# Value product of four head groups in one TensorE run, and attention weights loaded again for each chunk

## The chip, the cores and the metric

The kernel runs on one core of one Trainium2 chip. The metric is the time of one execution in microseconds (us), as the device measures it; the median of three runs of the kernel before is 558.66 us (558.55 to 558.71). A core has five engines that run side by side, each with an instruction stream of its own: TensorE (PE, matmuls; its weight loads are listed as PEld), VectorE (DVE), ScalarE (ACT), GpSimd (POOL) and SyncE (SP). Transfers are issued here by SP and POOL and carried by 16 DMA engines. TensorE writes to PSUM, which the kernel treats as four units of 1024 fp32 columns, two banks each.

## What is computed

```python
xn = layernorm(x)                                   # x: [1, 2048, 576]
qkv = xn @ wqkv                                     # 32 heads of 18
scores = q @ k^T * 18 ** -0.5, only for 0 <= i - j < 256
o = softmax(scores) @ v
s = concat(o) @ wo
h = sigmoid(xn @ w_gate) * (xn @ w_up)              # [2048, 4608]
g = silu(h @ w_down)
out = x + s * g
```

All tensors are bf16. The gated feed-forward part has eight times the width of the attention part and takes most of the matmul time.

## The kernel before

The 2048 rows are worked in four chunks of 512 (`NT`). For each chunk the builder makes operations, each with an engine, an estimated duration, dependencies and a priority: layer norm and transposition of the input (`build_ln`), the v projection (`build_v`), the q/k projection in five column groups (`build_qk`, `NQK` = 5), attention in eight head groups of four heads (`build_attn`), the output projection (`build_wo`), and the feed-forward part (`build_ffn`: 36 gate/up tiles `f1`, then `f2` in quarters of four tiles). `schedule` then puts all operations into one fixed order per engine with a model of durations and transfers, and `emit` writes the streams with the waits between them. The feed-forward matmuls of one chunk are laid between the attention work of that chunk and the next, so that TensorE has work while ACT and DVE treat the scores.

Nearly all matmuls are issued by `pair` (L122): two row tiles of 64 rows, each with 128 weight columns, side by side in the array.

*Attention of one head group.* Five score operations (`sc`) fill PSUM; ACT takes the exponential into a slot of the ring `expr` (L751, `NEX` = 12 slots), DVE multiplies the mask into it (L764). The exponentials stay transposed, keys on the partitions. The ring `qk` has `NQS` = 4 slots for the spread-out q and k of a head group.

*The value product.* After every second head group, `build_pv` makes one operation `pv` of 96 matmuls (64 in chunk 0, which has no earlier keys), L801. They are 64 rows by 19 columns of weights (18 values of v and a column of ones that yields the softmax sum), two row tiles by four column tiles: eight matmuls for each of 12 (8) blocks of keys. The results lie in one PSUM unit. DVE transposes each half out of PSUM (L819), takes the reciprocal of the sums (L822), multiplies (L823) and transposes back (L827); SP and POOL then move the rows into `oT` for the output projection. `ot1`, the fp32 transposed result, is a buffer of its own. There are four such runs in a chunk, 16 in the kernel.

*Weights.* wqkv and wo are loaded once, at the start or, for wo, after the first value run, and stay in SBUF (`wqk`, `wqkr`, `wv_sb`, `wvr`, `wo_sb`, `wor`); the last q/k group has its columns copied together into `wq4` by DVE. The 64 first rows of every weight (`...r`) lie apart from the other 512. Gate and up weights stream through a ring of four slots in every chunk; w_down is loaded in chunk 0 and stays.

*Order and PSUM.* `pool_s` (units 0 and 1) serves scores, projections and value products, `pool_f` (units 2, 3, 1) the feed-forward part. `schedule` picks for each engine the operation that can start first, with a small weight for its priority, and gives TensorE operations the unit that comes free first. `emit` places a wait ahead of an operation for each semaphore that is not yet known to have reached its value; what an instruction can't carry itself stands in the stream as an instruction that only waits.

The lines that matter below: L122 (`pair`), L801 (value product), L819 to L827 (its drain on DVE), L949 (the DVE half of an `f1` tile, which frees its PSUM unit), L1077 to L1174 (`schedule`).

Of the kernel before, what the change touches and what calls it, by code (L numbers as in the profile page):

```python
# [34 lines left out]
NQS = 4  # L35
NKX = 2
NEX = 12
OENG = ("SP", "POOL")
PV_ORDER = (0, 5, -4, -3, -2, -1, 1, 2, 3, 4, 6, 7)
TURN_NS = 265.0  # L40
BINS = (((-4, 0, 1), (1, 1, 5), (6, 6, 2)),
# [12 lines left out]
NXR = 2  # L54
# [135 lines left out]
class Op:  # L190
    __slots__ = ("eng", "est", "deps", "fn", "name", "prio", "start", "end", "tok", "needs_tok",
                 "nbytes", "slack", "idx", "succs", "cidx", "odeps", "acq", "lane", "filler", "space")

    def __init__(self, eng, est, fn, name, deps, prio, nbytes, odeps, acq):
# [30 lines left out]
        self.space = 0.0  # L225
        for d in self.odeps:
            assert d.eng == eng
# [22 lines left out]
class Builder:  # L250
# [17 lines left out]
    def op(self, eng, est, fn, name="", deps=(), prio=3, nbytes=0, odeps=(), acq=None):  # L268
        o = Op(eng, est, fn, name, deps, prio, nbytes, odeps, acq)
        o.cidx = len(self.ops)  # L270
        self.ops.append(o)
        for d in o.deps:
            d.succs.append(o)
        for d in o.odeps:
            d.succs.append(o)
        return o
# [12 lines left out]
    def alloc_memory(self):  # L289
# [30 lines left out]
        self.ot1, _ = seq("ot1", [P, 1, NT], f32)  # L320
# [4 lines left out]
        self.wqk, _ = seq("wqk", [P, KB - 1, 2, D])  # L325
        self.wqkr, _ = seq("wqkr", [P, D])
        self.wq4, _ = seq("wq4", [P, KB, 2, RD])
        self.wv_sb, _ = seq("wv_sb", [P, KB - 1, D])
        self.wvr, _ = seq("wvr", [P, D // 2])
        self.wo_sb, _ = seq("wo_sb", [P, KB - 1, D])  # L330
        self.wor, _ = seq("wor", [P, D // 2])
        self.qd, _ = seq("qd", [P, NQD, 2, NT])
        self.xr, _ = seq("xr", [P, NXR, D])
# [21 lines left out]
        self.pool_f = Pool("F", [2, 3, 1], last)  # L355

    def build_graph(self):
        self.r_xr = Ring(NXR, "xr")
# [6 lines left out]
        self.r_ot1 = Ring(1, "ot1")  # L365
# [21 lines left out]
        self.x_dma = {}  # L387
        self.op_wgr = {}
        self.q_slot = {}
        self.op_sp = {}  # L390
        self.sp_grp = {}
        self.hg_grps = {}
# [3 lines left out]
        for c in range(NC):  # L396
            self.build_ln(c)
            if c == 0:
                self.build_attn_consts()
            self.build_v(c)  # L400
            made = 0
            for hg in range(NHG):
                need = min(NQK, (4 * DH * (hg + 2) - 1) // P + 1)
                while made < need:
                    self.build_qk(c, made)
                    made += 1
                self.build_attn(c, hg)
            self.build_wo(c)
            self.build_ffn(c)

    def load_x(self, c, i=0):
# [8 lines left out]
        for _ in range(2):  # L420
            s_, d_ = self.r_xr.produce()
            slots.append(s_)
            dd += d_
        assert slots[1] == slots[0] + 1
        o = self.dma(self.xr[:, slots[0]:slots[0] + 2, :],
# [3 lines left out]
        for j in range(2):  # L429
            self.x_dma[st + j] = (o, self.xr[:, slots[j], :])  # L430
# [9 lines left out]
    def build_consts(self):  # L440
# [17 lines left out]
        wq, wk, wv = (self.wqkv[:, i * D:(i + 1) * D] for i in range(3))  # L458
        self.op_wqk = [self.load_nat(self.wqk[:, :, i, :], w, "dma:wqk", ("wqk", i), 5) for i, w in enumerate((wq, wk))]
        self.op_wqk += self.load_rem(self.wqkr[:, :], (wq, wk), "dma:wqkr", ("wqkr",), 5)  # L460
        for o in self.op_wqk:
            o.slack = 2500.0
        self.op_wv = [self.load_nat(self.wv_sb[:, :, :], wv, "dma:wv", ("wv",), 6)]
        self.op_wv += self.load_rem(self.wvr[:, :], (wv[:, 0:288], wv[:, 288:D]), "dma:wvr", ("wvr",), 6)
        for o in self.op_wv:
            o.slack = 5000.0
        self.op_wqk4 = [op("DVE", 420, lambda e: e.tensor_copy(self.wq4[:, 1:KB, :, :], self.wqk[:, :, :, 512:D]), "init:wq4",
                           deps=self.op_wqk, prio=2)]
        for t in range(2):
            for i in range(2):  # L470
                self.op_wqk4.append(op("DVE", 130, lambda e, t=t, i=i: e.tensor_copy(
                    self.wq4[ROWS[t], 0, i, :], self.wqkr[ROWS[1 - i], 512:D]), f"init:wq4:{t}{i}", deps=self.op_wqk, prio=2))

    def warm(self, n, dep, before, est):
# [5 lines left out]
        for i in range(n):  # L480
            w = self.op("PE", est, f_warm, f"warm:{i}", deps=[dep], prio=4, acq=None if before else h, odeps=[before])
# [27 lines left out]
    def build_ln(self, c):  # L509
# [3 lines left out]
        for i in range(BPC):  # L513
# [24 lines left out]
            sn, dn = self.r_xn.produce()  # L538
# [17 lines left out]
            if c:  # L556
                self.r_xr.release(i % 2, ap)
# [11 lines left out]
            tr = op("PE", KB * 29.5, f_tr, f"tr:{st}", deps=[ap, dup, self.op_ident, war], prio=0, acq=h)  # L569
# [37 lines left out]
    def halves(self, h, n):  # L607
        b = h.units[0] * 1024
# [6 lines left out]
    def build_qk(self, c, gi):  # L615
# [6 lines left out]
        gc = slice(gi * P, (gi + 1) * P)  # L622

        def lhs(r, t, k):
            if gi == 4:
                return self.wq4[r, k, :, :].rearrange("p i c -> p (i c)")
            return self.wqk[r, k - 1, t, gc] if k else self.wqkr[r, gc]
# [4 lines left out]
        pj = self.two("qk", f"{c}:{gi}", n, h, lhs, rhs, [self.op_xnT[c], self.op_wqk if gi < 4 else self.op_wqk4, dq], n)  # L632
# [8 lines left out]
        for u in range(H):  # L641
# [12 lines left out]
            for w, (dst, src) in enumerate(moves):  # L654
                o = self.dma(dst, src, n_ * 2 * NT * 2 // len(moves), f"dma:sp:{c}:{u}:{w}:{gi}", ("qk", par, gi),
# [3 lines left out]
                self.sp_grp.setdefault((c, gi), []).append(o)  # L659
                self.r_qd.release(sq, o)  # L660
            self.hg_grps.setdefault((c, hg), set()).add(gi)

    def two(self, kind, tag, est_n, h, lhs, rhs, deps, n, prio=1):
        lo = None
        for hi in range(2):
            def f(eng, hi=hi):
                return turn(eng, self.halves(h, n), lhs, rhs, hi)
            lo = self.op("PE", len(BLOCKS[hi]) * mm_ns(est_n), f, f"{kind}{hi}:{tag}", deps=[lo] if hi else deps, prio=prio,
                         acq=None if hi else h)
# [7 lines left out]
    def build_v(self, c):  # L677
        op = self.op
        xs = c % 2
        for i in range(BPC):  # L680
# [5 lines left out]
            vp = self.row_proj("v", st, h, lambda r, k, cols=cols: self.xnT[r, xs, k, cols], self.wv_sb, self.wvr,  # L686
                               [self.op_xnT[c][i], self.op_wv, war])
            self.xnT_rel[c].append(vp)
            self.op_v[st] = []
# [14 lines left out]
    def build_attn(self, c, hg):  # L704
        op = self.op
        qs = self.q_slot[(c, hg)][0]
        sp = [o for gi in sorted(self.hg_grps[(c, hg)]) for o in self.sp_grp[(c, gi)]]
# [18 lines left out]
        for vi, (specs, groups) in enumerate(zip(bins, masks)):  # L726
# [3 lines left out]
            def f_sc(eng, specs=specs, h=h):  # L730
                res = None
                outs = self.halves(h, NT)
                for ks, q0, nq in specs:
# [7 lines left out]
                    deps=[sp, kxo, self.r_ex.rel[self.r_ex.uses % NEX]], prio=1, acq=h, odeps=[self.last_vis])  # L741
# [30 lines left out]
        if hg % 2:  # L772
            self.build_pv(c, hg // 2)
        if (c, hg) == (0, 1):
            pv = self.op_pv[(c, hg)]
            self.op_wo_w = [self.load_nat(self.wo_sb[:, :, :], self.wo, "dma:wo", ("wo",), 8, [pv])]
            self.op_wo_w += self.load_rem(self.wor[:, :], (self.wo[:, 0:288], self.wo[:, 288:D]), "dma:wor", ("wor",), 8, [pv])

    def build_pv(self, c, pr):
        op = self.op  # L780
        pend, self.pend = self.pend, []
        hp = self.pool_s.hold()
# [3 lines left out]
        span = {ks: (max(ks, 0), min(ks + 5, SPC)) for ks in kss}  # L786

        def f_pv(eng):
            res = None
            outs = self.halves(hp, NT)  # L790
            for n, ks in enumerate(kss):
                q0, q1 = span[ks]
                cols = slice(q0 * SW, q1 * SW)
                for g, (hg, where, _) in enumerate(pend):
                    se = where[(ks, q0)]
                    assert all(where[(ks, q)] == se for q in range(q0, q1))
                    for t in range(2):
                        o = sub_pos(c, ks) * VSZ + (2 * hg + t) * VH
                        p0 = 32 * (2 * g + t)
                        for i in range(2):  # L800
                            res = eng.matmul(outs[i][p0:p0 + VH, cols], self.v_aug[ROWS[i], o:o + VH],  # L801
                                             self.expr[ROWS[i], se, t, cols], start=n == 0, stop=n == len(kss) - 1,
                                             tile_position=(64 * i, p0), skip_group_check=True)
            return res
        est = TURN_NS + sum(mm_ns((b - a) * SW) for a, b in span.values())
        pv = op("PE", est, f_pv, f"pv:{c}:{pr}", deps=[[m for _, _, rd in pend for m, _ in rd], vdeps], prio=1, acq=hp)
        for hg, _, rd in pend:
            self.op_pv[(c, hg)] = pv
            for se in sorted({se for _, se in rd}):
                self.r_ex.release(se, pv)  # L810
        for i in range(2):
            p1, d1 = self.r_ot1.produce()
# [5 lines left out]
            def f_t1(e, i=i, p1=p1):  # L818
                return e.transpose(self.ot1[:, p1, :], self.halves(hp, NT)[i])  # L819
            t1 = op("DVE", dve_ns(NT), f_t1, f"ot:{c}:{pr}:{i}", deps=[pv, d1], prio=1)  # L820
            hp.release(t1)
            rc = op("DVE", 255, lambda e, o1=o1: e.reciprocal(o1[:, :, DH], o1[:, :, DH]), f"rc:{c}:{pr}:{i}", deps=[t1], prio=1)  # L822
            on = op("DVE", dve_ns(NT // 32 * DH), lambda e, o1=o1, o2=o2: e.tensor_tensor(  # L823
                o2[:, :, 0:DH], o1[:, :, 0:DH], o1[:, :, DH:VH].broadcast_to([P, NT // 32, DH]), ALU.mult),
                f"on:{c}:{pr}:{i}", deps=[rc, d2, self.op_o2z], prio=1)
            self.r_ot1.release(p1, on)
            t2 = op("DVE", dve_ns(NT), lambda e, p2=p2, p3=p3: e.transpose(self.o2T[:, p3, :], self.o2[:, p2, :]),  # L827
                    f"ot2:{c}:{pr}:{i}", deps=[on, d3], prio=1)
# [26 lines left out]
    def build_wo(self, c):  # L855
        op = self.op
        last = []
        for i in range(BPC):
# [7 lines left out]
            wo = self.row_proj("wo", qb, h2, lambda r, k, cols=cols: self.oT[r, k, cols], self.wo_sb, self.wor,  # L866
                               [self.op_o[c], self.op_wo_w, war])
# [404 lines left out]
```

## Time and profile before

| | |
|---|---|
| median of three runs | 558.66 us |
| profiled execution, its own time | 558.58 us |
| span of its profile, first to last instruction | 557.2 us |
| instructions in the profile | 19237 |
| L801 matmuls | 1408, in 16 runs |
| L819 transposes out of PSUM | 32, 700 ns mean, 22.4 us in all |
| L949 | 144, 683 ns mean, 98.2 us in all |
| L751 exponentials | 160, 969 ns mean, 154.8 us in all |
| main DMA queue (q1) | 105960 packets, 60.68 MB, 40.1% of 16 engines |
| all DMA | 67.83 MB, mean 122 GB/s |

A row of the timeline gives the start and the length of a group of equal instructions in us, the engine, the line, the operation, what it writes and reads, the shape and how many there are. The length of a matmul row runs to the modelled end of its last matmul, and matmuls overlap in the pipeline; so what a stretch costs TensorE is read from start to start, not from the lengths. A bracket at the end gives the idle time of the engine before the row and what ended it.

### The profile page before, as it was taken

How to read it: one execution, taken by the hardware profiler on the slowest of the kernel's cores; microseconds unless marked ns; L12 is line 12 of the kernel's file. 1: busy time of each engine (PE TensorE's matmuls, PEld its weight loads, DVE VectorE, ACT ScalarE, POOL GpSimd, SP SyncE). 2: the span in 40 equal slices, each digit the busy share in tenths (PEclk: the TensorE clock that was granted, in tenths of full speed). 3: DMA queues.
4: the chain of work that ended last, by engine and by line, in shares of the span. 5: the costliest groups of instructions: out<-in, count | busy, mean ns of one | idle time of the engine just before them, and what ended most of it. 6: DMA issues, size and time to landing. Idle time of an engine off the chain costs nothing.

```text
span 557.2 us, 19237 instructions
## 1 busy us (share of the span) xinstructions
PE 552.6 (99%) x8342; PEld 339.1 (61%) x8342; DVE 328.4 (59%) x787; ACT 274.9 (49%) x379; POOL 210.1 (38%) x360
## 2 busy tenths in 40 slices
PE   8999999999999999999999999999999999999998
PEld 7454444677755545457886555645588754444787
DVE  5477788787568667674558857357567523333111
ACT  4245654443656655645656464565656433333201
POOL 5564456566245454440667444034382200000000
DMA  7988987931125535434121264234511035542010
GB/s 222 309 244 191 230 257 218 204 61 45 51 75 155 160 107 147 142 108 96 28 63 45 70 191 125 84 113 140 168 38 38 23 105 156 171 144 75 2 44 25
DMA packets 113468, 67.83 MB, mean 122 GB/s; under 512 B 18620, under 2 KB 111516, under 8 KB 113384
## 3 DMA queue, kind: packets, MB, share of 16 engines
q1 hardware_dynamic: 105960, 60.68, 40.1%
q0 software_dynamic: 7424, 5.92, 4.0%
q8 instruction: 66, 1.08, 0.8%
q14 instruction: 18, 0.15, 0.1%
HBM read 55.15 MB, written 2.36 MB: 103 GB/s over the span
## 4 chain that ended last, share of the span: by engine, by line
PE 98%; DVE 1%; DMA 0%; issue 0%; ACT 0%
PE ps L122 95%; PE ps L801 3%; DMA x<-in_A_x_dram 0%; DVE small L525 0%; DVE small L527 0%; DVE xnr L541 0%; PE ps L599 0%; DVE xnr L545 0%; ACT thf L1059 0%; DVE small L529 0%; DVE small L531 0%; DVE thf L1061 0%; DVE xf L1064 0%
## 5 line engine op out<-in xcount | busy, mean ns | idle before, releaser
L122 PE MATMUL ps<-xnT,wgs 64*128 64x512 bf16 (+1 forms) x2400 | 282.6, 368 | 0.2
L751 ACT ACTIVATE expr<-ps 128x1024 bf16<-128x1024 f32 (+4 forms) x160 | 154.8, 969 | 77.8 <-PE ps L122 77.2
L122 PEld LDWEIGHTS ps<-xnT,wgs 64*128 64x128 bf16 x2400 | 113.8, 94 | 115.1 <-DVE hT L949 1.6
L122 PE MATMUL ps<-wd_sb,hT 64*128 64x288 bf16 (+2 forms) x2448 | 156.7, 276 | 0.0
L949 DVE SCALAR_TENSOR_TENSOR hT<-tring,ps 128x512 bf16<-128x512 bf16 x144 | 98.2, 683 | 94.8 <-ACT tring L946 93.7
L946 ACT ACTIVATE tring<-ps 128x512 bf16<-128x512 f32 x144 | 86.1, 598 | 129.8 <-PE ps L122 127.6
L122 PEld LDWEIGHTS ps<-wd_sb,hT 64*128 64x128 bf16 x2448 | 112.5, 94 | 28.4
L279 POOL DMA_DIRECT2D qk<-qd x160 | 82.2, 521 | 119.8 <-PE ps L122 109.6
L764 DVE TENSOR_TENSOR expr<-expr,mask 128x128 bf16<-128x128 bf16 (+2 forms) x240 | 63.2, 297 | 62.1 <-ACT expr L751 61.6
L715 POOL TENSOR_SCALAR kx<-kprev,small 128x256 bf16<-128x256 bf16 x64 | 61.3, 967 | 28.2 <-PE ps L122 27.4
L122 PE MATMUL ps<-qk,kx 64*128 64x320 bf16 (+1 forms) x704 | 59.4, 254 | 0.0
L279 POOL DMA_DIRECT2D oT<-o2T x72 | 36.4, 513 | 58.7 <-DVE o2T L827 49.8
L122 PE MATMUL ps<-xnT,wgr 64*128 64x512 bf16 (+1 forms) x300 | 55.9, 367 | 0.0
L122 PEld LDWEIGHTS ps<-qk,kx 64*128 64x128 bf16 x704 | 31.2, 94 | 21.6 <-ACT expr L751 0.6
L122 PE MATMUL ps<-xnT,wqk 64*128 64x512 bf16 x256 | 32.6, 376 | 0.0
L819 DVE STREAM_TRANSPOSE ot<-ps 128x512 f32<-128x512 f32 x32 | 22.4, 700 | 11.6 <-PE ps L801 11.6
L715 DVE TENSOR_SCALAR kx<-qk,small 128x512 bf16<-128x512 bf16 x64 | 22.3, 378 | 4.7 <-PE ps L122 4.1
L122 PEld LDWEIGHTS ps<-xnT,wgr 64*128 64x128 bf16 x300 | 14.9, 94 | 16.6
L827 DVE STREAM_TRANSPOSE o2T<-o 128x512 bf16<-128x512 bf16 x32 | 22.7, 711 | 1.0
L637 DVE CAST qd<-ps 128x1024 bf16<-128x1024 f32 (+1 forms) x20 | 22.1, 1110 | 1.5 <-PE ps L122 1.5
L697 ACT ACTIVATE v_aug<-ps 64x288 bf16<-64x288 f32 x32 | 13.1, 409 | 17.3 <-PE ps L122 16.8
L801 PEld LDWEIGHTS ps<-expr,v_aug 64*19 64x19 bf16 x1408 | 17.2, 87 | 6.0 <-issue 3.3
(72 smaller groups left out, 291.5 us busy)
## 6 DMA issues: line engine op xcount, KB each, us to landing
wgs<-in_B_w_gate_dram SPq DMA_DIRECT2D x72, 256.0 KB, 3.4
wgs<-in_B_w_up_dram SPq DMA_DIRECT2D x72, 256.0 KB, 3.8
wd_sb<-in_B_w_down_dram SPq DMA_DIRECT2D x9, 576.0 KB, 6.3
qk<-qd POOLq DMA_DIRECT2D x100, 36.0 KB, 2.6
wgr<-in_B_w_gate_dram SPq DMA_DIRECT2D x36, 64.0 KB, 2.2
wgr<-in_B_w_up_dram SPq DMA_DIRECT2D x36, 64.0 KB, 2.4
xf<-in_A_x_dram SPq DMA_DIRECT2D x16, 144.0 KB, 2.9
out_dram<-xf SPq DMA_DIRECT2D x15, 144.0 KB, 1.8
```

Source lines behind the costliest of these rows:

```text
L122: res = eng.matmul(outs[i], lhs(ROWS[t], i), rhs(ROWS[t], i), start=start, stop=stop, tile_position=(64 * t, 0))
L279: o = self.op(eng, DMA_ISSUE_NS[eng], lambda e: e.dma_start(dst, src), name, deps, prio, nbytes=nbytes)
L637: return eng.tensor_copy(dst, self.both(h, n))
L697: return eng.activation(dst, src, ACTF.Copy)
L715: return e.tensor_scalar(self.kx[:, sx, pos:pos + n_ // SW, t, :], src.rearrange("p (s k) -> p s k", k=SW), self.half[:, t:t + 1], None, A ...
L751: return eng.activation(self.expr[:, se, :, lo * SW:NT], self.both(h, NT)[:, :, lo * SW:NT], ACTF.Exp, scale=SM_SCALE)
L764: return eng.tensor_tensor(e_, e_, m_, ALU.mult)
L801: res = eng.matmul(outs[i][p0:p0 + VH, cols], self.v_aug[ROWS[i], o:o + VH], self.expr[ROWS[i], se, t, cols], start=n == 0, stop=n == len( ...
L819: return e.transpose(self.ot1[:, p1, :], self.halves(hp, NT)[i])
L827: t2 = op("DVE", dve_ns(NT), lambda e, p2=p2, p3=p3: e.transpose(self.o2T[:, p3, :], self.o2[:, p2, :]), f"ot2:{c}:{pr}:{i}", deps=[on, d3 ...
L946: th = op("ACT", act_ns(NT), lambda e: e.activation(self.tring[:, st, :], bank(h, 0), ACTF.Tanh, scale=0.5), f"th:{c}:{ft}", deps=[pg, dt_ ...
L949: mu = op("DVE", dve_ns(NT), lambda e: e.scalar_tensor_tensor(self.hT[:, ft, :], self.tring[:, st, :], 1.0, bank(h, 1), ALU.add, ALU.mult) ...
```

## The change

Three things change together.

The value product is made once for four head groups (`PVG` = 4): two operations of 96 (64) matmuls that stand directly behind each other in TensorE's order (`then`), in a hold of two PSUM units from a pool `pool_v` over all four units. Both units are released when all four transposes of the two parts are done. There are two such runs in a chunk, eight in the kernel. `expr` has 20 slots instead of 12, and `ot1` now uses the same ring's numbering and the memory of the same slots. The priorities of L822 to L827 go from 1 to 2.

The scheduler counts TensorE's instructions as it places them (`at`, two for each matmul: its weight load and itself, given by `ni`). The first part of a value run is placed only where its middle would lie within 10 instructions (40 in chunk 0) of 193 past a multiple of 256 by this count.

The buffers of the weights and the input change as well: q/k weights are loaded for each column group of each chunk into a ring of two (`load_wq`), v and o weights share one buffer and are loaded for each chunk (`load_vo`), the separate input buffer `xr` goes (the input is loaded into `xnr` and normalised in place), and the ring of q/k slots has three instead of four. A q/k group is projected one head group later than before, and attention waits only for the moves of its own head group.

```diff
-NQS = 4
+NQS = 3
-NEX = 12
+NEX = 20
+NWQ = 2
+PVG = 4
+FETCH = 256
+FETCH_AT = 193
+FETCH_OFF = 10
+FETCH_OFF0 = 40
...
+        self.ot1 = nc.alloc_sbuf_tensor_at("ot1", [P, NEX, NT], f32, offset=zex)
...
+        self.pool_v = Pool("V", [0, 1, 2, 3], last)
...
-                need = min(NQK, (4 * DH * (hg + 2) - 1) // P + 1)
+                need = min(NQK, (4 * DH * (hg + 1) - 1) // P + 1)
...
+    def load_wq(self, c, gi):
+        sw, dw = self.r_wq.produce()
+        wq, wk = (self.wqkv[:, i * D:(i + 1) * D] for i in range(2))
+        w = P if gi < 4 else RD
+        both = self.wqkv[:, 0:2 * D].rearrange("r (i c) -> r i c", i=2)[:, :, gi * P:gi * P + w]
+        main = self.wqg[:, sw, :, 0:2 * w].rearrange("p k (i c) -> p k i c", i=2)
+        ds = [self.dma(main[:, :, i, :], both[RD:D, i, :].rearrange("(k p) c -> p k c", p=P), (D - RD) * w * 2, f"dma:wq:{c}:{gi}:{i}",
+                       ("wqg", sw, i), deps=dw, prio=5) for i in range(2)]
...
+    def load_vo(self, c, w, name, deps):
+        ds = [self.load_nat(self.wvo[:, :, :], w, f"dma:{name}:{c}", (name,), 6, deps)]
+        ds += self.load_rem(self.wvor[:, :], (w[:, 0:288], w[:, 288:D]), f"dma:{name}r:{c}", (name + "r",), 6, deps)
...
     def build_v(self, c):
+        wv = self.load_vo(c, self.wqkv[:, 2 * D:3 * D], "wv", [self.wo_last])
...
-        if hg % 2:
-            self.build_pv(c, hg // 2)
+        if hg % PVG == PVG - 1:
+            self.build_pv(c, hg // PVG)
...
+    def build_pv(self, c, run):
         op = self.op
         pend, self.pend = self.pend, []
-        hp = self.pool_s.hold()
+        hold = self.pool_v.hold(PVG // 2)
...
+        for n in range(PVG // 2):
+            pair2 = pend[2 * n:2 * n + 2]
...
+            est = (0.0 if n else TURN_NS) + sum(mm_ns((b - a) * SW) for a, b in span.values())
+            before = pv
+            pv = op("PE", est, f_pv, f"pv:{c}:{run}:{n}", deps=[] if n else deps, prio=1, acq=None if n else hold, odeps=[before],
+                    ni=16 * len(kss))
+            if before:
+                before.then = pv
+            else:
+                pv.off = 16 * len(kss) * (PVG // 2) // 2
...
+            self.build_o(c, run * (PVG // 2) + n, hold, n, pv)
+
+    def build_o(self, c, pr, hp, un, pv):
         for i in range(2):
-            p1, d1 = self.r_ot1.produce()
+            p1, d1 = self.r_ex.produce()
...
             def f_t1(e, i=i, p1=p1):
-                return e.transpose(self.ot1[:, p1, :], self.halves(hp, NT)[i])
+                return e.transpose(self.ot1[:, p1, :], self.halves(hp, NT, un)[i])
             t1 = op("DVE", dve_ns(NT), f_t1, f"ot:{c}:{pr}:{i}", deps=[pv, d1], prio=1)
             hp.release(t1)
...
     def build_wo(self, c):
+        wo_w = self.load_vo(c, self.wo, "wo", [self.v_last])
...
     def schedule(self):
+        at = 0
+        nxt = None
...
                 for o in cand:
+                    if e == "PE" and nxt is not None and o is not nxt:
+                        continue
+                    if o.off is not None:
+                        d = (at + o.off - FETCH_AT + FETCH // 2) % FETCH - FETCH // 2
+                        if abs(d) > (FETCH_OFF if o.off > FETCH // 2 else FETCH_OFF0):
+                            continue
...
             if o.eng == "PE":
+                at += o.ni
+                nxt = o.then
```

## The prediction

> **What bounds the kernel now.** I read the busy shares first, then the chain that ended last, then the matmuls around one value run in order of time, then the instruction fetches.
>
> ```profile
> PE 552.6 (99%) x8342; PEld 339.1 (61%) x8342; DVE 328.4 (59%) x787; ACT 274.9 (49%) x379; POOL 210.1 (38%) x360
> ...
> PE 98%; DVE 1%; DMA 0%; issue 0%; ACT 0%
> ```
>
> TensorE is busy all the time and is nearly all of the chain. No other engine passes 60%. So only what shortens or holes TensorE's own stream counts, and every moved load or drain is free as long as TensorE does not run out of work for it. The granted clock is 1.00 throughout. The program after has the same 8342 matmuls, so the gain can only be in how they follow each other.
>
> The rows at one value run in chunk 1 (L801) and at one in chunk 0:
>
> ```profile
> 162.68 1.03 PE L122 MATMUL ps<-xnT,wgs 64*128 64x512 bf16 x8
> 163.54 0.38 PE L122 MATMUL ps<-xnT,wgr 64*128 64x512 bf16 x2
> 163.85 1.34 PE L801 MATMUL ps<-expr,v_aug 64*19 64x320 bf16 x96
> 165.13 0.40 PE L122 MATMUL ps<-qk,kx 64*128 64x64 bf16 x6
> ...
> 62.54 1.03 PE L122 MATMUL ps<-xnT,wgs 64*128 64x512 bf16 x8
> 63.40 0.38 PE L122 MATMUL ps<-xnT,wgr 64*128 64x512 bf16 x2
> 63.71 1.01 PE L801 MATMUL ps<-expr,v_aug 64*19 64x320 bf16 x64
> 64.65 0.39 PE L122 MATMUL ps<-qk,kx 64*128 64x320 bf16 x4
> ```
>
> Read the starts. Four pairs of 512 columns take 163.54 - 162.68 = 0.86 us, so a pair costs 0.215 us (0.42 ns a column). The last pair before a run takes 0.31: the way into a run costs 0.095 us. The run itself takes 1.28 us from its first start to the next matmul in chunks 1 to 3, and 0.94 us in chunk 0. Its columns alone (2560 and 1920, eight tiles at a time) are 1.075 and 0.806 us at 0.42 ns. All twelve runs of chunks 1 to 3 take 1.27 to 1.28 us in the trace's records, all four of chunk 0 take 0.94.
>
> The loads of weights show why the way in costs something:
>
> ```profile
> 163.33 0.10 PEld L122 LDWEIGHTS ps<-xnT,wgr 64*128 64x128 bf16 x2
> 163.85 1.19 PEld L801 LDWEIGHTS ps<-expr,v_aug 64*19 64x19 bf16 x96 [0.42 <-issue]
> ```
>
> Elsewhere a weight load starts under the matmul before it. Here none starts until the array has changed from two tiles of 64x128 to eight of 64x32. That is the turn, paid 16 times now and 8 times after.
>
> **The change part by part.** *Fewer turns.* In the records the last block of 8 matmuls of a run takes 178 ns (144 in chunk 0) to the next matmul, 122 ns of it after its last matmul; followed by another block of the same tiles I expect 68 (28): the records show eight matmuls 8 to 9 ns apart once the queue is drained, 3 to 4 ns apart in chunk 0. That saves 110 (116) ns. With it go the 95 ns in, about 7 ns in the first block, and 10 ns at the second pair after a run. Against it, the second half of a joined run in chunks 1 to 3 starts with a drained queue, so its narrow blocks are bound by issue (28 ns becomes about 68): 35 ns back. A join saves 0.19 us in chunks 1 to 3 and 0.226 in chunk 0. There are 6 and 2 of them: 6 x 0.187 + 2 x 0.226 = 1.57 us. Bounds: only the way in, 8 x 0.095 = 0.76; everything over the bare columns (0.296 and 0.229 a join), 2.23.
>
> *The two-unit hold.* A joined run takes two of the four PSUM units and gives both back after its fourth L819 transpose (700 ns mean). In chunks 1 to 3 the next claimant stands 1.94 to 2.16 us of TensorE work behind the run (f1 halves of 0.86 and 1.08, f2 quarters of 0.49); in chunk 0, 2.45 and 3.02. The DVE order puts the four transposes together. They begin some 0.2 us after the first half of the run ends (1.2 us before the joined run does), or after the L949 before them, and need 2.9 us: released 1.9 to 2.1 us after the run. Two runs, the first of chunk 1 and the last of chunk 3, come about 0.13 us short; I charge 0.27 us. Behind the claimant queue only matmuls in TensorE's fixed order, so a late release is a hole. If one L949 (683 ns) slipped between the transposes, each of the six later runs would lose about 0.6. Bounds: 0 to 3.6.
>
> *Loads.* SP issues 456 transfers instead of 362, POOL the same 356. The weights of 2.7 MB come again in three chunks, 8 MB on 67.8, and q/k in rows of 256 B: some 20,000 more packets. A packet of the main queue costs 40.1% x 16 x 557 / 105960 = 34 ns of one of 16 engines, so the packets cost 11 us of all engines per chunk of 139 us, against a DMA share of 0.41 in 139 to 270 us and 0.37 in 270 to 400. In the first 60 us the share is 0.86, but there the queue now carries q/k in parts as they are needed, and f1 weights move up: counting bytes of the queue against its packet ends, f1 weights land 5 to 16 us ahead of their first matmul from 20 to 70 us. Hidden: 0. If that cover were gone, a stall would be of the order of one landing, 3.4 us for a gate weight. The o weights now wait for v's last matmul and v's for o's; v is due only at the next value run, tens of us later. In-place normalising and three q slots lengthen waits on SP and POOL, which TensorE does not see while the score order holds. The init copies to wq4 leave DVE (1 us, off the path).
>
> *Where the runs' middles really stand.* Queue q8 fetches TensorE's instructions:
>
> ```profile
> q8 instruction: 66, 1.08, 0.8%
> ```
>
> 66 fetches of 16 KB is one per 256 instructions over 2 x 8342 = 16,684 loads and matmuls plus 219 instructions that only wait. Set against the stream's position, the fetch times fit best with an edge at 193 past each multiple of 256 *if the waiting instructions are counted*. The scheduler's count `at` adds only `ni`, so it drifts; the program after holds 260 such waits. Counted in full, the eight middles lie +30, +34, +103, +135, -102, -56, -38 and -9 instructions from the nearest edge. So the change mostly does not do what it says: three runs (both of chunk 1, the first of chunk 2) hold two edges, 256 apart; the others one.
>
> What that costs depends on how far ahead blocks are fetched, which this trace does not show: its closest edges are about 4 us apart, and no run waits. In runs of the trace a fetch starts 1.1 to 1.6 us after the edge is passed and takes 0.9 to 1.4: landed after 2.0 to 2.7 us. TensorE, some 42 instructions behind its sequencer, needs 298 instructions x 6.1 ns = 1.8 us to use up what it has. If only one block is ahead, three runs lose 0.2 to 0.9 us each, 0.6 to 2.7 in all, about 1.7. If more are ahead, 0. I take 0, since in no row has TensorE waited for a block, even where a fetch came 5 us after its edge; but both ends stay in the range.
>
> The Trainium skill, "Runtime: NRT & Kernel Launch", section "Instruction fetch mechanics", says that blocks of 256 are prefetched in sequence and hidden because an engine issues no faster than about 20 cycles an instruction. The row speaks against the reason: 192 instructions in 1.28 us is 6.7 ns. The same section gives a buffer of two blocks in one sentence and 2,048 instructions for TensorE in another; by the first the sum would be the rival's below, by the second the forecast's.
>
> **Sum.** The profiled execution took 558.58 us (span 557.25 and 1.33 around it), 0.08 under the median of 558.66. 558.58 - 1.57 + 0.27 = 557.28; on the median 557.36, say 557.3.
>
> **The rivals.** *Turn gain eaten by fetch.* One block ahead, three runs short: 557.36 + 1.7 = 559.1 (558.0 to 560.1). For it: the landing times and the missed edges. Against it: no wait for a block in the trace. It is slower than before by over 0.2% from 0.8 us a run, that is from landings 2.6 us after the edge.
>
> *Slower: the drain behind a joined run.* Place: the first claim after each of the six runs of chunks 1 to 3. If one L949 stands ahead of a transpose the hole is about 0.6 us: 557.1 + 3.6 = 560.7. It decides from 0.45 us a run (1.57 + 1.1 over 6). For it: margins of 0 to 0.2 us, while one-unit runs left 3.0 to 4.3. Against it: the order puts the four transposes first.
>
> *Late loads.* 256 B rows land later than planned and TensorE waits once or twice for a q/k part: 557.4 + 1 to 2 = 558.9. Against it: the landing margins above.
>
> **How the numbers follow.** Forecast 0.52, fetch 0.30, drain 0.10, late loads 0.08. A measurement of this kernel can't tell less than about 0.2% (1.1 us) from no change. The forecast's own range is 556.4 to 557.9 and is beyond 0.2% with 0.45 of its 0.52. The fetch rival gives 0.03 faster, 0.17 the same, 0.10 slower; the drain 0.10 slower; late loads 0.05 same and 0.03 slower. Together: faster 0.48, same 0.29, slower 0.23. The range runs from 556.4 to 559.9, which leaves out the drain and the upper part of the fetch case.
>
> **What would show it.** Eight value runs: their first start to the next matmul near 2.47 us (twice 1.28 less 0.11 and 0.007, plus 0.035; 1.76 in chunk 0), and 0.31 before each. If the fetch rival is right, the three runs with two edges are longer by 0.2 to 0.9 us than the three others, with a gap near instruction 294 to 345 of 384, right where the second fetch lands. If the drain is, TensorE idles before the first score behind a run, released by L819's successor. Late loads would show as waits on a DMA. I am wrong if TensorE's busy time outside the value runs changes, or if a join saves under 0.1 us.

## The result, and the profile after

| | before | after |
|---|---|---|
| median | 558.68 us (558.55 to 558.89, 4 runs) | 566.08 us (565.75 to 569.93, 4 runs) |
| ratio, 95% interval | | 1.0148 (1.0104 to 1.0191) |
| span of the profile | 557.2 us | 564.8 us |

The change makes the kernel slower by about 7.4 us. The busy shares of after and the shares of the chain that ended last:

```profile
PE 553.2 (98%) x8342; PEld 340.6 (60%) x8342; DVE 324.4 (57%) x782; ACT 272.1 (48%) x379; POOL 207.8 (37%) x360
...
PE 97%; issue 1%; DVE 1%; DMA 0%; ACT 0%
```

TensorE does the same 8342 matmuls in nearly the same busy time (552.6 us before), so the loss is idle time between matmuls. "Issue" has grown from 0% to 1% of the chain: TensorE stood still, and nothing that the profile records was late. The view of the waits, by engine and line (what was waited for, us in total, times, longest), says where:

```profile
PE ps L816 <- issue: 6.2, 3, 2.8
```

L816 is the value product. Three waits, none of them for another engine. The timeline of TensorE at two joined runs without a wait (the second of chunk 2, the first of chunk 0) and at two of the three with one (first of chunk 1, second of chunk 1):

```profile
374.64 2.47 PE L816 MATMUL ps<-expr,v_aug 64*19 64x320 bf16 x192
377.05 1.04 PE L127 MATMUL ps<-xnT,wgs 64*128 64x512 bf16 x8
...
86.39 1.86 PE L816 MATMUL ps<-expr,v_aug 64*19 64x320 bf16 x128
88.19 1.04 PE L127 MATMUL ps<-xnT,wgs 64*128 64x512 bf16 x8
...
196.09 2.35 PE L816 MATMUL ps<-expr,v_aug 64*19 64x320 bf16 x172
201.27 0.37 PE L816 MATMUL ps<-expr,v_aug 64*19 64x256 bf16 x20 [2.82 <-issue]
201.57 1.05 PE L127 MATMUL ps<-xnT,wgs 64*128 64x512 bf16 x8
202.44 0.60 PE L127 MATMUL ps<-xnT,wgr 64*128 64x512 bf16 x2
202.84 1.92 PE L127 MATMUL ps<-xnT,wgs 64*128 64x512 bf16 x8
204.54 0.64 PE L127 MATMUL ps<-qk,kx 64*128 64x64 bf16 x6
...
254.53 2.11 PE L816 MATMUL ps<-expr,v_aug 64*19 64x320 bf16 x156
258.46 0.64 PE L816 MATMUL ps<-expr,v_aug 64*19 64x320 bf16 x36 [1.82 <-issue]
```

Read from start to start. A joined run takes 2.41 us where nothing holds it (2.56 as two runs before) and 1.80 in chunk 0 (1.88 before). The stalled ones stop behind 172 and 156 matmuls. Behind the longest stop there is a second loss: eight matmuls of 512 columns, which take 0.87 us from 201.57 to 202.44, take 1.70 from 202.84 to 204.54. The view by windows (us, busy time and count of PE, PEld, DVE, ACT and POOL, granted clock, DMA share, GB/s) has the reason:

```profile
201.40:206.00 4.60, 4.60 (x50) 1.99 (x37) 3.22 (x6) 1.37 (x2) 0.00 (x0) 0.63 0.01 4
```

The granted clock is 0.63 in this stretch; in the records it is 0.5 for one piece of 3.41 us, from 202.47 to 205.88, and 1.0 up to the end of the work otherwise.

The three stops, set against the fetches of TensorE's instructions (queue q8). "Passed" is when its sequencer passed the edge in the first half of the run, worked out from the position in the stream with the sequencer 42 instructions ahead of the matmuls; fetch and stop are rows of the trace, us; "stop" is the start of the last matmul ahead of it, and the last column counts the instructions of the run up to there, two for each matmul:

```
run            passed   fetch starts  landed   stop     goes on   stop lasts   at instruction
chunk 1, 1st   196.34   198.76        199.74   198.17   201.27    3.09         344 of 384
chunk 1, 2nd   254.55   255.70        256.96   256.34   258.46    2.12         312
chunk 2, 1st   313.12   314.27        315.39   315.10   316.97    1.87         294
```

The second edges of these runs were worked out beforehand at 345, 313 and 294. So each fetch brings the block behind the next edge, and TensorE stops at that edge until the block can be used, which is 1.5 to 1.6 us after it has landed.

What the half clock costs can be read from the starts: the work from 202.44 to 206.08 takes 3.63 us; its eight pairs of 512 columns at 0.215 us and its score operation at 0.22 take 1.94 at full clock, so 1.7 us are lost.

The time is nearly all accounted for: stops 7.03 us over what those matmuls cost otherwise, half clock 1.7, some more small holes 0.7, and 1.9 gained by the joins, 7.5 in all; the spans differ by 564.8 - 557.2 = 7.6.

### The profile page after: what moved, and what is told of

Its sections match the earlier page's. It is cut to its first block, busy times and chain, and to the rows that moved or that the text cites. A ratio compares the mean times of both kernels' runs of the same rounds, so it can differ in the third digit from the quotient of the medians.

```text
span 564.8 us, 19415 instructions
## 1 busy us (share of the span) xinstructions
PE 553.2 (98%) x8342; PEld 340.6 (60%) x8342; DVE 324.4 (57%) x782; ACT 272.1 (48%) x379; POOL 207.8 (37%) x360
## 4 chain that ended last, share of the span: by engine, by line
PE 97%; issue 1%; DVE 1%; DMA 0%; ACT 0%
PE ps L127 94%; PE ps L816 3%; DMA x<-in_A_x_dram 0%; DVE small L540 0%; DVE small L542 0%; DVE xnr L556 0%; PE ps L612 0%; DVE xnr L560 0%; ACT thf L1086 0%; DVE small L544 0%; DVE small L546 0%; DVE thf L1088 0%; DVE xf L1091 0%
## 5 line engine op out<-in xcount | busy, mean ns | idle before, releaser
L127 PEld LDWEIGHTS ps<-xnT,wgs 64*128 64x128 bf16 x2400 | 112.5, 94 | 116.9 <-issue 2.6
L127 PEld LDWEIGHTS ps<-wd_sb,hT 64*128 64x128 bf16 x2448 | 115.0, 94 | 26.8
L779 DVE TENSOR_TENSOR expr<-expr,mask 128x128 bf16<-128x128 bf16 (+2 forms) x240 | 64.9, 297 | 72.2 <-ACT expr L766 70.8
L730 POOL TENSOR_SCALAR kx<-kprev,small 128x256 bf16<-128x256 bf16 x64 | 59.9, 946 | 11.5 <-PE ps L127 10.6
L127 PE MATMUL ps<-xnT,wqg 64*128 64x512 bf16 (+1 forms) x320 | 37.8, 355 | 0.0
L844 DVE STREAM_TRANSPOSE ot<-ps 128x512 f32<-128x512 f32 x32 | 20.4, 688 | 16.8 <-PE ps L816 16.8
L816 PE MATMUL ps<-expr,v_aug 64*19 64x320 bf16 (+4 forms) x1408 | 19.3, 254 | 6.2 <-issue 6.2
L816 PEld LDWEIGHTS ps<-expr,v_aug 64*19 64x19 bf16 x1408 | 16.9, 86 | 10.3 <-issue 9.1
```

Of the source, the lines that this page charges most:

```text
L127: res = eng.matmul(outs[i], lhs(ROWS[t], i), rhs(ROWS[t], i), start=start, stop=stop, tile_position=(64 * t, 0))
L730: return e.tensor_scalar(self.kx[:, sx, pos:pos + n_ // SW, t, :], src.rearrange("p (s k) -> p s k", k=SW), self.half[:, t:t + 1], None, A ...
L779: return eng.tensor_tensor(e_, e_, m_, ALU.mult)
L844: return e.transpose(self.ot1[:, p1, :], self.halves(hp, NT, un)[i])
```

## The experiments

Theory A: two edges of the fetch blocks follow each other faster than a block can be fetched and made ready. Rivals: the joined run itself (its length, its hold of two PSUM units), the reloaded weights, and whatever else the rings moved.

**e1: the scheduler counts the instructions that only wait.** The whole change stays; only the count becomes right, so that each run's middle really lies on an edge.

```diff
-        at = 0
+        at = 2
...
+                        pick = o.acq.pool.pick(o.acq.n, max(free[e], ready_t[o.cidx]))
+                        extra = len(waits(o, pick[1])) // 2 if pick else 0
-                        d = (at + o.off - FETCH_AT + FETCH // 2) % FETCH - FETCH // 2
+                        d = (at + extra + o.off - FETCH_AT + FETCH // 2) % FETCH - FETCH // 2
...
-                at += o.ni
+                w_ = waits(o)
+                known.update(w_)
+                at += o.ni + len(w_) // 2
```

> The changed kernel with the scheduler's count made to include the instructions that only wait, so that the middles of all eight value runs lie within 10 instructions of an edge in chunks 1 to 3 and within 30 in chunk 0. Theory A (one block is fetched ahead, and a run with two edges stalls at the second): no gap over 0.2 us inside any value run, granted clock 1.00, and the eight joins save 6 x 0.25 + 2 x 0.19 = 1.9 us against the kernel before: 556.8 us, at most 557.6. Theory B (the loss comes from the weights that are loaded again and the smaller rings): still 563 to 566 us, since none of that is changed. Theory C (the two-unit hold): also still slow, with idle TensorE behind the runs.

Measured: 559.87 us (558.96 to 561.7, 12 runs), ratio 1.0017 (1.0008 to 1.0026). All eight joined runs go through without a stop, as this one of chunk 1 in the timeline of e1; but a stop remains behind another, in `f2`:

```profile
192.71 2.47 PE L816 MATMUL ps<-expr,v_aug 64*19 64x320 bf16 x192
195.11 1.04 PE L127 MATMUL ps<-xnT,wgs 64*128 64x512 bf16 x8
...
252.17 0.28 PE L127 MATMUL ps<-wd_sb,hT 64*128 64x288 bf16 x1
253.27 1.64 PE L127 MATMUL ps<-wd_sb,hT 64*128 64x288 bf16 x23 [0.82 <-issue]
```

About 6.2 of the 7.4 us come back by the count alone. The time is still 2.3 us above theory A's upper bound of 557.6: in the profile stand two stops behind runs (1.10 and 0.43 us) and some 3 us of small holes, which e7 comes back to. This profile is of the slowest of the twelve executions (561.7 us), so the median one holds less of them. The stop behind 252.17 is at the next edge after a run that ended at 250.25: the edge before it was passed in the middle of the run, at 248.83, the fetch started at 250.75 and landed at 251.82, and TensorE went on at 253.27, 1.45 us later. So the rule is not about runs: a block takes so long, whatever work reaches its edge first.

**e2: the reloads and rings alone.** Runs of two head groups as before, placed anywhere.

```diff
-PVG = 4
+PVG = 2
...
-                pv.off = 16 * len(kss) * (PVG // 2) // 2
+                pv.off = None
```

> The changed kernel with value runs of two head groups again (16 runs, one PSUM unit each, placed anywhere); the weights loaded again for each chunk, the rings and the priorities stay as changed. Theory A: 558.7 us, between 558.3 and 559.5, value runs of 1.28 and 0.94 us as before, clock 1.00. Theory B: 563 us or more. Theory C: 558.7.

Measured: 559.22 us (558.3 to 560.32, 12 runs), ratio 1.0006 (0.9997 to 1.0016). The reloads are not what costs 7 us. Their own price, 0.65 us by the medians, can't be told from nothing. The profile, of the slowest of the twelve (560.32 us), has two single waits. One fetch in its profile, outside the value runs, started 4.67 us after its edge and stopped TensorE for 0.64 us, 1.58 after landing to the next matmul. And one value run of chunk 0 waited 1.0 us for the mask product (L779), where the kernel before has no such wait.

**e3: as many edges as possible.** e1 with the target half a block further on, so that each of the six runs of chunks 1 to 3 holds two edges, some 68 and 324 instructions in.

```diff
-FETCH_AT = 193
+FETCH_AT = 193 + 128
```

> As e1_waits_counted, but every joined run is placed half a block off: all six runs of chunks 1 to 3 hold two edges (some 68 and 324 instructions in), the two of chunk 0 (256 instructions) one each. Theory A: six gaps of 1.9 to 3.1 us just ahead of instruction 324 of the run, 11 to 19 us together, and a stretch of 3.4 us at half clock (1.7 us lost) behind the longest ones: 568 to 585 us, middle 574. Theories B and C: no more than the changed kernel's 566.

Measured: 573.44 us (571.97 to 575.48, 4 runs), ratio 1.0261 (1.0236 to 1.0287). All six runs stop at the second edge, for 2.28, 2.25, 1.39, 2.71, 1.56 and 2.40 us. The longest, in the timeline of e3:

```profile
370.77 1.71 PE L816 MATMUL ps<-expr,v_aug 64*19 64x256 bf16 x118
374.90 0.63 PE L816 MATMUL ps<-expr,v_aug 64*19 64x320 bf16 x34 [2.41 <-issue]
375.46 0.40 PE L127 MATMUL ps<-qk,kx 64*128 64x64 bf16 x6
375.70 3.70 PE L127 MATMUL ps<-xnT,wgs 64*128 64x512 bf16 x16
```

The clock behind it, in the view by windows of e3 (columns as above):

```profile
375.70:379.10 3.40, 3.34 (x20) 0.99 (x18) 3.00 (x6) 1.02 (x1) 0.00 (x0) 0.50 0.02 5
```

The sixteen matmuls at 375.70 take 3.53 us at a clock of 0.50; 1.7 would be usual. The same work with the same loads, aimed half a block further on, goes from 559.87 to 573.44, and the six stops make up 12.6 of these 13.6 us. The time is the middle of theory A's range; two of the six stops (1.39 and 1.56) are shorter than the 1.9 that it gave as the least. That all six runs stop, at the place that was named, is the most direct evidence for theory A.

**e4: the first edge moved in steps.** e1 with the edge -5, 8, 17, 25, 34 and 38 instructions into the six runs, the second 256 further on.

```diff
+FIRST_EDGE = {(1, 0): -4, (1, 1): 4, (2, 0): 12, (2, 1): 20, (3, 0): 28, (3, 1): 36}
...
-                        d = (at + extra + o.off - FETCH_AT + FETCH // 2) % FETCH - FETCH // 2
+                        d = (at + extra + o.first - FETCH_AT + FETCH // 2) % FETCH - FETCH // 2
```

> As e1_waits_counted, but the first edge of the six runs of chunks 1 to 3 lies at -5, 8, 17, 25, 34 and 38 instructions from the run's start (the second 256 later). Theory A1 (the next block is usable a fixed 3.8 to 4.8 us after the sequencer, some 42 instructions ahead, passes the first edge): the gap grows by degrees, 0 to 0.5 us at -5, 0.5 to 1.2 at 8 to 17, 1.5 to 2.5 at 25 to 38; together 6 to 9 us, 563 to 566 us. Theory A2 (any run that holds both edges stalls by about the same 2 us): nothing at -5 and five gaps of 1.9 to 3.1 us, 567 to 574 us.

Measured: 564.41 us (564.2 and 564.61), ratio 1.0097 (1.0076 to 1.0118). The stops are 0.91, 0.84, 0.67, 0.62, 0.41 and 2.34 us: neither growing step by step, as A1 had it, nor all alike, as A2 had it. That the time lies in A1's range is luck. The place within the run alone does not set the length. What differs is the fetch: it started 2.67, 0.90, 1.19, 0.64, 0.22 and 1.80 us after its edge was passed, and TensorE went on 1.29 to 1.56 us after it landed, in all six.

**e5: joined only among `f1` work,** where an instruction takes longer, so that neighbouring edges are further apart in time. Five of the eight runs came out joined, the other six halves apart.

```diff
+                        calm = all(x[:2] == "f1" for x in ffn[-1:]) and int(ffn[-1].split(":")[2]) <= 35
+                        o.join = calm or o.off <= FETCH // 2
...
-                nxt = o.then
+                nxt = o.then if o.join else None
```

> As e1_waits_counted, but in chunks 1 to 3 the two halves of a value run are joined only where f1 matmuls (54 ns an instruction) stand around them, with the edge 187 to 242 instructions into the run; elsewhere the halves stand apart as two runs of 192 instructions. Five of eight runs are joined, three of them in chunks 1 to 3. Theory A (one block ahead; usable about 1.45 us after it has landed, 3.2 to 5 us after the edge before it is passed): gain of the joins 3 x 0.25 + 2 x 0.19 = 1.1 us; by the order one pair of edges (first run of chunk 3, some 3.4 us apart) still stalls by 0.4 to 1.1 us, the others not: 558.6 - 1.1 + 0.7 and up to 0.5 of turns within f1 = 558.3, between 557.3 and 559.3, and below e1_waits_counted's 559.9. Rival (the rest of e1_waits_counted's loss lies in the reloads and rings, 0.65 us by e2_reload_alone, not in fetches behind the runs): 559 to 560.

Measured: 559.9 us (559.1 to 560.75, 9 runs), ratio 1.0026 (1.0016 to 1.0036). This misses what theory A expected and lies in the rival's range, 559 to 560, though not for the rival's reason alone: two joined runs still stop, for 0.92 and 0.44 us. The longer one, in the timeline of e5:

```profile
188.74 1.57 PE L817 MATMUL ps<-expr,v_aug 64*19 64x320 bf16 x117
191.04 1.05 PE L817 MATMUL ps<-expr,v_aug 64*19 64x64 bf16 x75 [0.73 <-issue]
```

Here the fetch started 3.25 us after the edge was passed (at 185.41), landed at 189.60, and TensorE went on at 191.04. One edge inside the run is not safe either when a fetch starts that late. Besides, holes ahead of other matmuls add up to 2.2 us in this profile against 0.7 before. The largest is 0.65 us, behind the first run of chunk 0, where an `f1` tile waits for the last transpose (L845) of the held units; e7 comes back to the others.

**e6: joined, placed anywhere.**

```diff
-                pv.off = 16 * len(kss) * (PVG // 2) // 2
+                pv.off = None
```

> The changed kernel without its rule of placement. By position (waiting instructions counted) the first edge at or ahead of the eight runs' starts, in instructions from the start, and the next: -49 and 207; -11 and 245 (chunk 0, 256 long); -3 and 253; 45 and 301; -55 and 201; -47 and 209; 160 and 416 (32 behind the end); 45 and 301. Theory A: stalls just ahead of the second edge of about 0.5 (second run), 0.9 (third), 2.1 (fourth), 1 (seventh, behind its end), 2.1 (eighth), none in the first, fifth and sixth: 6.6 us together, between 4 and 9; 558.6 - 1.9 + 6.6 + 0.7 = 564, between 561.5 and 567. Rival (stalls have another cause than the edges): no tie to these places.

Measured: 565.87 us (565.0 and 566.73), ratio 1.0133 (1.0114 to 1.0151). The time is in theory A's range. The long stops are 2.12, 2.07 and 1.24 us in the fourth, eighth and third run, where 2.1, 2.1 and 0.9 were expected, and 0.61 behind the seventh, where 1 was. One of 0.55 us is in the first run, where none was expected; its fetch started 3.75 us after the edge. So the placing in the change, with its wrong count, is worth nothing: 566.08 with it, 565.87 without any.

**e7: everything kept but the join.** The second half of a run stands 35 to 66 instructions behind the first; one hold of two units spans both.

```diff
-                nxt = o.then
+                if o.then is not None:
+                    ready_t[o.then.cidx] = stt + o.est + 1500.0
```

> All of the change stays (one hold of two units for four head groups, the rings, the reloads, the placing of a run's middle by the uncounted position), except that the second half of a value run stands 35 to 66 TensorE instructions behind the first instead of directly behind it. The edges still fall as in the changed kernel: in the first run of chunk 1 at +87 and +343 instructions from the run's start, in the second at +55 and +311, in the first of chunk 2 at +12 and +268. Theory A (a block can be used 3.7 to 4.9 us after TensorE's sequencer passes the edge before, so it is the time between two edges that counts): between the two edges lie now two f1 halves more (1.94 us by the starts of the rows before), so that the second edge of the first run is reached some 3.8 us after the first is passed, of the second run 3.5 to 5, of the third about 5: stalls of 0 to 1.1, 0 to 1.2 and 0 in place of 3.09, 2.12 and 1.87, and no half clock. All 16 halves 1.28 us (0.94 in chunk 0) but for those. Joins give nothing any more: 558.6 + 0.65 for reloads and rings + 0 to 2 = 559.2 to 561.3. Rival H (what is lost behind the stalls is the hold: two PSUM units kept for the whole of both halves, up to four transposes late): the holes stand ahead of the first claim behind a run, released by a DVE transpose, 0.3 to 0.6 us behind each of six runs: 561 to 563. Rival J (the stall belongs to 384 instructions of these tiles in one row, wherever the edges lie): no stall in any half, 559.2.

Measured: 561.98 us (561.29 to 563.06, 4 runs), ratio 1.0066 (1.0049 to 1.0083), above theory A's range and inside rival H's. The timeline of e7 tells them apart; this is the first value run of chunk 1:

```profile
197.04 1.34 PE L816 MATMUL ps<-expr,v_aug 64*19 64x320 bf16 x96
198.32 1.04 PE L127 MATMUL ps<-xnT,wgs 64*128 64x512 bf16 x8
...
200.36 0.95 PE L816 MATMUL ps<-expr,v_aug 64*19 64x320 bf16 x57
201.81 0.65 PE L816 MATMUL ps<-expr,v_aug 64*19 64x320 bf16 x39 [0.50 <-issue]
202.39 1.04 PE L127 MATMUL ps<-xnT,wgs 64*128 64x512 bf16 x8
...
204.03 0.61 PE L127 MATMUL ps<-xnT,wgs 64*128 64x512 bf16 x4 [0.17 <-DVE ot L844]
```

The stop is at the same edge as in the changed kernel, in the middle of a half of 96 matmuls, and lasts 0.79 us in place of 3.09, since two `f1` halves now lie between the edges; the other two runs with two edges don't stop. So it is the time between two edges (against J, which left no stop in any half). What the hold does is the last row: one wait of 0.17 us for a transpose (L844), the only one in this profile. H's holes of 0.3 to 0.6 us behind six runs are not there. The time above A's range is spread over some ten holes of 0.1 to 0.3 us ahead of `f1`, score and output-projection matmuls (about 2.4 us in all, 0.7 before). I have not traced them to one cause; e1 (3.1), e3 (2.5), e4 (2.5) and e5 (2.2) have them too, e2 fewer (0.8, besides its one wait of 1.0). Every program that groups by four has them, with or without the join; that the grouping makes them is argued from this and not shown. Two of them, 0.2 us each at 78.3 and 79.5 in after, stand in all of these programs ahead of the first value run, so no held unit makes those two.

## Why the prediction was wrong

*The step that failed is the fetch.* The prediction had the mechanism, the three runs and the places, priced it between 0 and 0.2 to 0.9 us a run, and took 0. "I take 0, since in no row has TensorE waited for a block" is the choice that failed, and for two reasons. First, around the value runs of before the closest edges are passed 3.2 to 3.4 us apart, and there the fetches started 0.6 to 1.6 us after the edge; so these rows could not show a wait, and their silence said nothing of edges 2 us apart. Second, there is a row with a wait. It stands in the start-up, where the prediction did not look; the timeline of weight loads in before:

```profile
10.36 0.62 PEld L122 LDWEIGHTS ps<-xnT,wgs 64*128 64x128 bf16 x21 [0.28 <-issue]
```

By the position in the stream, the load at 10.36 is the first instruction behind the second edge. The first edge was passed at 4.97, some 5 us earlier, its fetch started at 7.95 and landed at 9.03, and TensorE went on 1.33 us after that. This one row already held the late start, the wait after the landing, and the sign that only one block is fetched ahead. What the runs show in place of the 0: one block ahead, and stops of 3.09, 2.12 and 1.87 us.

*Its bounds were too low as well.* Term by term, as they were put: TensorE uses up what it has in 1.8 us; measured 1.83, 1.79 and 1.98 from passing one edge to stopping at the next. Landed after 2.0 to 2.7 us; measured 3.40, 2.41 and 2.27. The third term was not in the sum: from landing to the next matmul it took another 1.53, 1.50 and 1.57 us. 3.40 + 1.53 - 1.83 = 3.10, 2.41 + 1.50 - 1.79 = 2.12, 2.27 + 1.57 - 1.98 = 1.86: the three stops. With that term the rival would have stood at 1.7 to 2.4 us a run and 5.1 to 7.2 in all, not 0.6 to 2.7. The row at 10.36 is the one of before that shows it (1.33 us).

*The half clock* (1.7 us) was not thought of: the prediction has no term for the clock, which was 1.00 in before.

*Fewer turns: right, and larger.* A join saves 0.25 us in chunks 1 to 3 (2.56 - 2.41 from first start to next matmul, and 0.095 for the way in) and 0.19 in chunk 0, against 0.187 and 0.226: 1.9 us in place of 1.57. A joined run takes 2.41 us where 2.47 was added up, so the 35 ns charged for the second half's narrow blocks, and as much again, were not lost; in chunk 0 it takes 1.80 where 1.76 was added up.

*The two-unit hold: charged 0.27; nothing waited.* The view of who waits for a line, for the transposes out of PSUM in after:

```profile
L844 DVE STREAM_TRANSPOSE ot<-ps x32: 671/674/717, 87.7 to 488.6; 128x512 f32<-128x512 f32 x32
...
who waited for it (us, times):
```

The list is empty: no claimant was held up. The term was sized too high: in the three runs without a stop the last transpose ends 1.54 us after the run, not 1.9 to 2.1, because four of them follow each other in 2.5 us, not 2.9. They stand together in DVE's order, as the prediction had read, and the rival of the drain, 0.6 us behind each of the six later runs, is in no profile. Late releases do occur in single places. The second run of chunk 0 in e1 (DVE, then weight loads):

```profile
126.71 2.50 DVE L844 STREAM_TRANSPOSE ot<-ps 128x512 f32<-128x512 f32 x4
...
129.27 0.36 PEld L127 LDWEIGHTS ps<-wd_sb,hT 64*128 64x128 bf16 x8 [0.39 <-DVE ot L844]
```

There TensorE loses 0.27 us behind the transposes (and 0.30 just before, behind an exponential); e4 has the same two, e5 the 0.65 us in chunk 0, e7 the wait shown above.

*Loads: hidden, as taken.* The main queue has 27,744 more packets in after, not some 20,000, but TensorE waits for no transfer there, and e2 bounds the price of reloads and rings at 0.0016 of the time. (The profile of e1 has one wait for a gate weight, 0.71 us, at start-up.)

*How far ahead blocks are fetched.* The prediction had weighed two sentences of the Trainium skill, "Runtime: NRT & Kernel Launch", section "Instruction fetch mechanics". Here TensorE issued an instruction every 6 ns in the value runs and did stop for fetches, so the reason that the page gives for their being hidden does not hold for this engine; of its two sizes for the buffer, the runs fit the sentence that speaks of two blocks.

No version beat the kernel before. The joins give 1.9 us of 558.7, and e1 and e5, which of the joined versions lose the least to stops, give that back in the stops that are left and in small holes.

## What to carry to other kernels

Count the fetch blocks of an engine in time, not in instructions: find the edges by the queue that fetches them, with the instructions that only wait counted, and see that two edges are not closer than some 5 us, with a margin for a late start, where the instructions are short (6 ns each here, 1.6 us a block). That is an estimate from these stops, and no safe limit: where a fetch started 3.0 to 4.7 us after its edge, TensorE stopped at the next edge although it reached it only 5.1 (before), 5.7 (e6) and 6.8 us (e2) after passing the edge before. Look for a mechanism's sign in every stage of the trace, start-up too, before a term is put at nothing; and rows without a wait bound it only down to the spacing that they hold. And an order that depends on a position in the stream needs every instruction of the stream in its count, or it is no better than chance.

## What the runs showed of the hardware

*A block is usable late.* In the stops at an edge (0.3 to 3.1 us, 32 in the nine profiles) TensorE stood within two instructions of it and went on 1.2 to 1.6 us after the block had landed. The fetch itself took 0.9 to 1.6 us there. The part that varies is its start: 0.2 to 4.67 us after the edge was passed, where a stop followed. Over 248 fetches of after, e1, e3 and e4 the median delay is some 0.9 us where the DMA engines were under 20% busy around it and 2.2 to 2.5 where they were over 60% busy, by how wide a stretch is counted. That is a correlation; no run changed the traffic alone, and what happens between the landing and the next matmul no run shows.

*The clock drops by a window of its own.* The granted clock changes on a grid of 3.41 us. Counting TensorE's idle time in each piece of that grid after start-up, the three pieces with 2.0 us or more of it (2.2 in after; 2.0 and 2.4 in e3) are each followed by one at half clock, and none of those with 1.6 or less is, though e3 and e6 have stops of 2.1 to 2.4 us that lie across two pieces. (The start of e1 also has a piece at half clock, behind one with 1.6 us idle, which this does not explain.) So in mid-run it is not the length of a stop but how much of it falls into one piece. The Trainium skill, "TensorE: Matmul & The Clock Gate", Part 1, describes a free-running window of that length; the limit, between 1.6 and 2.0 us here, is from these runs alone. It fits the 3.09-us stop in after, which cost 1.7 us more, and the two 3.4-us pieces in e3's profile.
